# A layer's gradient passes through W2, W1 and Wo: products of rows already transposed first, row dots as soon as they can, the gelu slope made ahead, and the copies of these chains on ScalarE

## The chip, the cores and the metric

The kernel runs on one core of a Trainium2 chip. The metric is the time of one execution on the device, in microseconds (us). Lower is better. Each profile is of one run (for the kernel before, of one that is not in its median), so a trace's span and the median of the runs need not agree to the last microsecond.

The profile names the engines PE (TensorE matmuls), PEld (TensorE weight loads), DVE (VectorE), ACT (ScalarE), POOL (GpSimd) and SP (which issues loads).

## The reference

A decoder of four residual steps, attention, MLP, attention, MLP, with the same weights in both layers; then the gradient of everything by `grad_out`. There is one new token for each of two batch entries, so every matrix product has 2 columns, while the cache has 16384 positions. Cut to what matters:

```python
B, Sq, D = 2, 1, 1024;  Hq, Hkv, Sk, Dh = 32, 4, 16384, 128;  F = 3584

def attn(x, k_cache, v_cache, wq, wo):        # wq: D x 4096, wo: 4096 x D
    q = (x @ wq) ...                          # 32 heads, 8 to each cached head
    p = softmax(q k^T * Dh**-0.5)
    return (p v) ... @ wo
def mlp(x, w1, b1, w2, b2):
    y = layernorm(x)
    return gelu(y @ w1 + b1) @ w2 + b2

x = x + attn(layernorm(x), ...);  x = x + mlp(layernorm(x), ...)   # layer 0
x = x + attn(layernorm(x), ...);  x = x + mlp(layernorm(x), ...)   # layer 1
# outputs: x and, by jax.vjp, the gradients of x, k_cache, v_cache, wq, wo, w1, b1, w2, b2
```

## The kernel before

The kernel streams the caches through the core several times. Between the backward pass of layer 1's attention and the last stage (cache and weight gradients) lies a stretch in which one small vector, layer 0's gradient, must pass through everything in order:

- `dn` (the gradient that comes out of layer 1's attention), one layernorm backward, `gM_all`;
- W2 transposed (28 rows of 128), `dh_all`;
- W1 transposed, `dm_sb`;
- two layernorms backward, `gA_all`;
- Wo transposed (32 rows), `dof`, from which the last stage starts.

The weights lie in memory the wrong way round for this. A row of W2 or Wo is therefore "turned" first: eight 128x128 transposes on PE into an accumulator bank, one copy back by ScalarE or VectorE. Turning doesn't need the gradient, only the products of the row do. Every fifth row is not turned but "dotted": VectorE multiplies the row as it lies with the gradient spread over all partitions and sums, once for each batch entry. The spread itself is eight transposes and one copy for each batch entry. Rows of W2 have a second job, the forward product of layer 1 (into `fps`).

`pick` decides at build time which engine makes a copy: the one that has been charged less. The `hook` of `ln_bwd` puts PE work (rows to turn) into the wait for the cross-partition sum `part_sum`, which is itself a PE matmul.

```python
    load = {"A": 0.0, "D": 0.0}

    def charge(eng, us):
        load[eng] += us

    def pick():
        m = min(load.values())
        for k in load:
            load[k] -= m
        return "A" if load["A"] <= load["D"] else "D"

    def evac_bf16(dst, src, n):
        if pick() == "A":
            S.copy(out=dst.bitcast(I32), in_=src.bitcast(I32))
            charge("A", 0.17 + n / 2 / 1200.0)
        else:
            V.tensor_copy(out=dst, in_=src)
            charge("D", 0.16 + n / 1920.0)
    # ... cut ...
    def ln_bwd(dy, y, rstd, name, hook=lambda: None):
        t1 = wrk.tile([128, DJ, 2], F32, name="lb_t1")
        V.tensor_tensor(out=t1[:], in0=dy, in1=y, op=ALU.mult)
        s = small.tile([128, 2, 2], F32, name="lb_s")
        V.tensor_reduce(out=s[:, 0, :], in_=dy.rearrange("p j b -> p b j"), axis=AX.X, op=ALU.add)
        V.tensor_reduce(out=s[:, 1, :], in_=t1[:].rearrange("p j b -> p b j"), axis=AX.X, op=ALU.add)
        hook()
        ps = part_sum(s[:].rearrange("p a b -> p (a b)"), 4, "lb_ps")
        nm = small.tile([128, 2, 2], F32, name="lb_nm")
        V.tensor_scalar(out=nm[:].rearrange("p a b -> p (a b)"), in0=ps[:], scalar1=-1.0 / D, scalar2=None,
                        op0=ALU.mult)
        u = wrk.tile([128, DJ, 2], F32, name="lb_u")
        V.tensor_tensor(out=u[:], in0=y, in1=bcast_j(nm[:, 1, :], DJ), op=ALU.mult)
        V.tensor_tensor(out=u[:], in0=u[:], in1=dy, op=ALU.add)
        V.tensor_tensor(out=u[:], in0=u[:], in1=bcast_j(nm[:, 0, :], DJ), op=ALU.add)
        dx = wrk2.tile([128, DJ, 2], F32, name=name, tag="lb_dx")
        V.tensor_tensor(out=dx[:], in0=u[:], in1=bcast_j(rstd, DJ), op=ALU.mult)
        return dx
    # ... cut ...
    def turn(view, new_tp):

        tp = new_tp()
        for o in range(8):
            PE.transpose(tp[:, o, :], view[:, o * 128:(o + 1) * 128], ident[:])
        evac_bf16(view, tp[:].rearrange("p a b -> p (a b)"), 1024)

    class Dots:

        def __init__(self, name):
            self.rows = [ktp.tile([128, 2 * NB, 128], BF16, name=name, tag="blk", bufs=2) for _ in range(2)]
            self.junk = wrk.tile([128, D], BF16, name="junk", tag="rowout")

        def spread(self, b, col):
            tp = pt([128, 8, 128], BF16, "dotr")
            for o in range(8):
                PE.transpose(tp[:, o, :], col(o).to_broadcast([128, 128]), ident[:])
            evac_bf16(self.rows[b][:].rearrange("p a b -> p (a b)"), tp[:].rearrange("p a b -> p (a b)"), 1024)

        def dot(self, w, b, out):
            V.scalar_tensor_tensor(out=self.junk[:], in0=w, scalar=1.0, in1=self.rows[b][:].rearrange("p o d -> p (o d)"),
                                   op0=ALU.mult, op1=ALU.mult, accum_out=out)
            charge("D", 1.15)

    class Ahead:

        def __init__(self, W, n_in, name, xT_bf=None, fps=None):
            self.W, self.J, self.x, self.fps, self.name = W, n_in // 128, xT_bf, fps, name
            self.dotted = range(3, self.J, 5)
            self.dp = vec.tile([128, len(self.dotted), 2], F32, name=name + "_dp")
            self.chunks = list(w_chunks(n_in, D))
            self.rows = {}

        def load(self, k):
            j0, rb = self.chunks[k]
            wv = w_load(self.W, j0, rb, D)
            for j in range(rb):
                self.rows[j0 + j] = wv[:, j, :]

        def row(self, j):
            w = self.rows[j]
            if self.fps is not None:
                for jo in range(DJ):
                    PE.matmul(wide_out(self.fps, jo * WIDE), lhsT=w[:, jo * 128:(jo + 1) * 128],
                              rhs=wide_in(self.x[:, j, :]), start=False, stop=True, skip_group_check=True)
            if j not in self.dotted:
                turn(w, lambda: pt([128, 8, 128], BF16, "turn"))

        def spread(self, gT_bf):
            self.dd = Dots(self.name + "_g")
            for b in range(2):
                self.dd.spread(b, lambda o: gT_bf[:, o, b:b + 1])

        def products(self, j, out_ps, gT_bf):
            if j in self.dotted:
                for b in range(2):
                    self.dd.dot(self.rows[j], b, self.dp[:, self.dotted.index(j), b:b + 1])
                return
            for o in range(8):
                PE.matmul(wide_out(out_ps, 2 * j), lhsT=self.rows[j][:, o * 128:(o + 1) * 128],
                          rhs=wide_in(gT_bf[:, o, :]), start=(o == 0), stop=(o == 7))
    # ... cut ...
    def mlp_hidden_bwd(l, dhps, ahead=None):
        # ... cut: eight VectorE operations make the slope d1 of gelu from hpre and th ...
        V.tensor_tensor(out=dh_all[:, :, lsl(l)], in0=d1[:], in1=dhps[:], op=ALU.mult)
        if ahead is not None:
            V.tensor_tensor(out=dh_all[:, 3:FJ:5, lsl(l)], in0=d1[:, 3:FJ:5], in1=ahead.dp[:], op=ALU.mult)
    # ... cut ...
    charge("D", 2.0)
    g2 = attn_in_bwd(1, g3, dn1, lambda: some(rest, 2))
    V.tensor_copy(out=gM_all[:, :, lsl(0)], in_=g2[:])
    w2b.spread(gM_all[:, :, lsl(0)])
    some(rest, 6)
    dhps = px([128, 512], F32, "w2b_b")
    for j in range(FJ):
        some(rest, 1)
        w2b.products(j, dhps, gM_all[:, :, lsl(0)])
    mlp_hidden_bwd(0, pairs(dhps, FJ), w2b)
    x4 = mlp_out(1, fps[:, 0:DJ * WIDE].rearrange("p (j b) -> p j b", b=WIDE)[:, :, 0:2])
    sv = saved["m0"]
    _, dmps = w_pass(B_w1, D, F, "dm_ps", gT_bf=dh_all[:, :, lsl(0)],
                     mid=lambda: col_to_row_f32(x4, DJ, out_0.rearrange("b s d -> (b s) d"), "o0"))
    wob = Ahead(A_wo, HD, "wob")
    for k in range(len(wob.chunks)):
        wob.load(k)
    rest = deque(lambda j=j: wob.row(j) for j in range(wob.J - 4))
    dm = wrk.tile([128, DJ, 2], F32, name="dm_sb")
    V.tensor_copy(out=dm[:], in_=dmps[:])
    dn = ln_bwd(dm[:], sv["y2"][:], sv["rstd2"][:], "dn", lambda: some(rest, 4))
    dx = ln_bwd(dn[:], sv["y1"][:], sv["rstd1"][:], "dx", lambda: some(rest, 4))
    g1 = vec.tile([128, DJ, 2], F32, name="gM0")
    V.tensor_tensor(out=g1[:], in0=dx[:], in1=g2[:], op=ALU.add)
    V.tensor_copy(out=gA_all[:, :, lsl(0)], in_=g1[:])
    wob.spread(gA_all[:, :, lsl(0)])
    dops = px([128, 512], F32, "wob_b")
    for j in range(wob.J + 4):
        some(rest, 1)
        if j >= wob.J - 4 and j < wob.J:
            wob.row(j)
        if j >= 4:
            wob.products(j - 4, dops, gA_all[:, :, lsl(0)])
    TP = [pt([128, 8, 128], BF16, "tpm%d" % i) for i in range(2)]
    for t in TP:
        V.memset(t[:].bitcast(F32), 0.0)
    do_delta(0, pairs(dops, HQ), wob)
```

The copy of a turned row, when `pick` gives it to VectorE, lands in VectorE's order at the place where the row is turned, that is inside `ln_bwd` or ahead of the dots. In the timelines below VectorE works in the order of emission, so what stands behind such a copy waits with it. And a dot is emitted where the products of its row are, one row at a time.

Of the kernel before, what the change touches and what calls it, by code (L numbers as in the profile page):

```python
# [23 lines left out]
def kernel(  # L24
# [114 lines left out]

    def pick():  # L140
        m = min(load.values())
        for k in load:
            load[k] -= m
        return "A" if load["A"] <= load["D"] else "D"
# [73 lines left out]
    def ln_bwd(dy, y, rstd, name, hook=lambda: None):  # L218
# [6 lines left out]
        ps = part_sum(s[:].rearrange("p a b -> p (a b)"), 4, "lb_ps")  # L225
        nm = small.tile([128, 2, 2], F32, name="lb_nm")
# [109 lines left out]
    class Ahead:  # L336


        def __init__(self, W, n_in, name, xT_bf=None, fps=None):
            self.W, self.J, self.x, self.fps, self.name = W, n_in // 128, xT_bf, fps, name  # L340
            self.dotted = range(3, self.J, 5)
            self.dp = vec.tile([128, len(self.dotted), 2], F32, name=name + "_dp")
            self.chunks = list(w_chunks(n_in, D))
            self.rows = {}
# [20 lines left out]

        def products(self, j, out_ps, gT_bf):
            if j in self.dotted:
                for b in range(2):
                    self.dd.dot(self.rows[j], b, self.dp[:, self.dotted.index(j), b:b + 1])
                return  # L370
            for o in range(8):
                PE.matmul(wide_out(out_ps, 2 * j), lhsT=self.rows[j][:, o * 128:(o + 1) * 128],
                          rhs=wide_in(gT_bf[:, o, :]), start=(o == 0), stop=(o == 7))
# [210 lines left out]
    def attn_bwd(l, do_bf, dqT, dn, groups, ahead):  # L584
# [88 lines left out]
        while s < len(slots) + 2 or sch.busy():  # L673
            sch.s = s
            if s < len(slots):
# [3 lines left out]
                else:  # L679
# [3 lines left out]
                    if s % 3 == 2 and v_turns:  # L683
                        v_turns.popleft()()
# [103 lines left out]
    def mlp_hidden_bwd(l, dhps, ahead=None):  # L788
# [11 lines left out]
        d1 = wrk.tile([128, FJ, 2], F32, name="gb_d1")  # L800
        V.tensor_scalar(out=d1[:], in0=th[:], scalar1=1.0, scalar2=0.5, op0=ALU.add, op1=ALU.mult)
        V.tensor_tensor(out=d1[:], in0=d1[:], in1=x2[:], op=ALU.add)
        V.tensor_tensor(out=dh_all[:, :, lsl(l)], in0=d1[:], in1=dhps[:], op=ALU.mult)
        if ahead is not None:
            V.tensor_tensor(out=dh_all[:, 3:FJ:5, lsl(l)], in0=d1[:, 3:FJ:5], in1=ahead.dp[:], op=ALU.mult)
# [17 lines left out]
    def do_delta(l, dops, ahead=None):  # L823
        sv = saved[f"a{l}"]
        dof = wrk.tile([128, G, 8], F32, name="dof")
        for b in range(2):
            V.tensor_tensor(out=dof[:, b * HKV:(b + 1) * HKV, :].rearrange("p k r -> p (k r)"), in0=dops[:, :, b],
                            in1=sv["rbc"][:, b * HKV:(b + 1) * HKV, :].rearrange("p k r -> p (k r)"), op=ALU.mult)
            if ahead is not None:
                r_ = sv["rbc"][:, b * HKV:(b + 1) * HKV, :].rearrange("p k r -> p (k r)")  # L830
                V.tensor_tensor(out=dof[:, b * HKV:(b + 1) * HKV, :].rearrange("p k r -> p (k r)")[:, 3:HQ:5],
                                in0=ahead.dp[:, :, b], in1=r_[:, 3:HQ:5], op=ALU.mult)
# [55 lines left out]
    def attn_in_bwd(l, gT, dn, hook=lambda: None):  # L888
        sv = saved[f"a{l}"]
        dx = ln_bwd(dn[:], sv["y"][:], sv["rstd"][:], "dxa", hook)  # L890
# [12 lines left out]
    mlp_hidden(1, x3)  # L903

# [21 lines left out]

    charge("D", 2.0)
    g2 = attn_in_bwd(1, g3, dn1, lambda: some(rest, 2))
    V.tensor_copy(out=gM_all[:, :, lsl(0)], in_=g2[:])
    w2b.spread(gM_all[:, :, lsl(0)])  # L930
    some(rest, 6)
    dhps = px([128, 512], F32, "w2b_b")
    for j in range(FJ):
        some(rest, 1)
        w2b.products(j, dhps, gM_all[:, :, lsl(0)])
    mlp_hidden_bwd(0, pairs(dhps, FJ), w2b)
# [10 lines left out]
    dn = ln_bwd(dm[:], sv["y2"][:], sv["rstd2"][:], "dn", lambda: some(rest, 4))  # L947
    dx = ln_bwd(dn[:], sv["y1"][:], sv["rstd1"][:], "dx", lambda: some(rest, 4))
    g1 = vec.tile([128, DJ, 2], F32, name="gM0")
    V.tensor_tensor(out=g1[:], in0=dx[:], in1=g2[:], op=ALU.add)  # L950
    V.tensor_copy(out=gA_all[:, :, lsl(0)], in_=g1[:])
    wob.spread(gA_all[:, :, lsl(0)])
    dops = px([128, 512], F32, "wob_b")
    for j in range(wob.J + 4):
        some(rest, 1)
        if j >= wob.J - 4 and j < wob.J:
            wob.row(j)
        if j >= 4:
            wob.products(j - 4, dops, gA_all[:, :, lsl(0)])
# [358 lines left out]
    m = 0  # L1318
# [68 lines left out]
```

## Time and profile before

| | before |
|---|---|
| time, median (3 runs) | 1174.13 us (1173.18 to 1174.6) |
| bytes moved by DMA | 449.30 MB, 384 GB/s over the span |
| `dn` to `dh_all` (norm and W2) | 27.49 us |
| `dh_all` to `dm_sb` (W1) | 23.06 us |
| `dm_sb` to `gA_all` (two norms) | 5.99 us |
| `gA_all` to `dof` (Wo) | 22.71 us |
| `dof` to the end (last stage) | 419.5 us |

The last five rows are differences of start times in the timeline of VectorE. From the page of the kernel before, the span and the busy times of the engines:

```profile
span 1171.5 us, 39963 instructions
PE 967.2 (83%) x17565; PEld 738.7 (63%) x17565; DVE 639.2 (55%) x1342; ACT 562.9 (48%) x1412; POOL 63.7 (5%) x113
```

No engine is full over the whole span. The DMA is, in most of it (a share of 0.99 up to 660 us and 0.98 from 850 us to the end), and nearly so beside W2 and W1 (a share of 0.84 at 676 to 700 us, 1.00 at 700 to 722), but not beside Wo. Windows of the kernel before (columns as its first line says; PEclk is the granted TensorE clock as a share of full speed):

```profile
core 0: us, PE busy (x) PEld busy (x) DVE busy (x) ACT busy (x) POOL busy (x), PEclk, DMA share, GB/s
730.00:740.00 10.00, 9.84 (x184) 9.33 (x182) 6.83 (x11) 5.37 (x10) 0.00 (x0) 0.84 0.06 10
740.00:750.00 10.00, 7.09 (x194) 6.66 (x190) 9.72 (x17) 4.57 (x8) 0.00 (x0) 1.00 1.03 391
```

At 730 to 740 us almost nothing is loaded (a share of 0.06), since no buffer comes free before rows of Wo are done with: in the waits of SP the last load of Wo waits 16.5 us, for a dot. Time in this stretch is a chain of waits, not bandwidth. VectorE's timeline of the kernel before, from `dm_sb` on (start, duration, engine, line, operation, output and inputs; in brackets the idle time before it and what ended that):

```profile
723.27 0.17 DVE L946 COPY dm_sb<-dm_ps_b 128x16 f32<-128x16 f32 x1 [1.44 <-PE dm_ps_b L274]
...
723.79 0.69 DVE L151 COPY wt<-turn 128x1024 bf16<-128x1024 bf16 x1
725.18 0.69 DVE L151 COPY wt<-turn 128x1024 bf16<-128x1024 bf16 x1 [0.70 <-PE turn L315]
725.79 0.15 DVE L227 TENSOR_SCALAR lb_nm<-lb_ps 128x4 f32<-128x4 f32 x1
...
727.13 0.69 DVE L151 COPY wt<-turn 128x1024 bf16<-128x1024 bf16 x1
728.02 0.16 DVE L227 TENSOR_SCALAR lb_nm<-lb_ps 128x4 f32<-128x4 f32 x1 [0.20 <-PE lb_ps L178]
...
729.26 0.17 DVE L951 CAST gA_all<-gM 128x16 bf16<-128x16 f32 x1
730.30 0.69 DVE L151 COPY wob_g<-dotr 128x1024 bf16<-128x1024 bf16 x1 [0.87 <-PE dotr L328]
732.09 0.69 DVE L151 COPY wt<-turn 128x1024 bf16<-128x1024 bf16 x1 [1.10 <-PE turn L315]
733.65 0.69 DVE L151 COPY wt<-turn 128x1024 bf16<-128x1024 bf16 x1 [0.87 <-PE turn L315]
735.08 0.69 DVE L151 COPY wt<-turn 128x1024 bf16<-128x1024 bf16 x1 [0.73 <-PE turn L315]
735.68 1.22 DVE L332 SCALAR_TENSOR_TENSOR junk<-wt,wob_g 128x1024 bf16<-128x1024 bf16 x1
...
749.69 1.22 DVE L332 SCALAR_TENSOR_TENSOR junk<-wt,wob_g 128x1024 bf16<-128x1024 bf16 x1
751.03 1.03 DVE L962 MEMSET tpm<- 128x512 f32 x2
751.97 0.17 DVE L827 TENSOR_TENSOR dof<-wob_b,rbc 128x32 f32<-128x32 f32 x1
```

The twelve dots follow each other without a gap from 735.68 us to the memsets and `dof`, so VectorE is what ends last in Wo. What can be won is the start of the first dot, 6.42 us after `gA_all`. In those 6.42 us VectorE makes four copies and waits before each of them for PE to transpose (0.87, 1.10, 0.87 and 0.73 us). Only the first of them, of the spread, is one that the dots need from VectorE. In the norms the copy at 725.18 us stands ahead of `lb_nm` in the same way: it waits 0.70 us for a turn that has nothing to do with the norm.

In W2 it is PE that ends last. VectorE's timeline of the kernel before around W2:

```profile
672.72 0.17 DVE L877 TENSOR_TENSOR dn<-dn,dn_ps 128x16 f32<-128x16 f32 x1 [1.91 <-PE dn_ps L875]
...
676.42 0.17 DVE L929 CAST gM_all<-gA 128x16 bf16<-128x16 f32 x1
...
697.41 0.21 DVE L792 TENSOR_TENSOR gb_t<-th 128x56 f32<-128x56 f32 x1
...
700.21 0.21 DVE L803 TENSOR_TENSOR dh_all<-gb_d,w2b_b 128x56 bf16<-128x56 f32 x1 [1.17 <-PE w2b_b L372]
```

The gelu slope (first operation at 697.41 us, line L792) is done 1.17 us before PE's last product, for which `dh_all` waits. So the slope at this place costs nothing. PE in turn waits once for the gradient, in the waits of PE between 672 and 702 us (us in total, times, longest):

```profile
PE dotr L328 <- DVE gM_all L929: 1.5, 1, 1.5
```

### The profile page before, as it was taken

The numbers are of one execution on the slowest core, as the hardware profiler recorded it, in microseconds if no ns is written. First come the engines' busy times: TensorE is split into PE (matmuls) and PEld (weight loads), VectorE is DVE, ScalarE is ACT, GpSimd is POOL, SyncE is SP. The second block draws the span as 40 slices with busy tenths as digits, with TensorE's granted clock in tenths as the row PEclk, the third lists the DMA queues.
The fourth block names the chain that finished last, engine by engine and source line by source line (L and its number), as shares of the span: only waits on it lengthen the run. The fifth ranks groups of instructions, "written<-read, shape, count | busy, mean of one in ns | idle before, by whom it ended". The sixth has DMA issues, their size and how long they took to land. (4 is left out here: it accounts for less than half of the span.)

```text
span 1171.5 us, 39963 instructions
## 1 busy us (share of the span) xinstructions
PE 967.2 (83%) x17565; PEld 738.7 (63%) x17565; DVE 639.2 (55%) x1342; ACT 562.9 (48%) x1412; POOL 63.7 (5%) x113
## 2 busy tenths in 40 slices
PE   4989796487879976899987788688898989999885
PEld 3867674487767755887775688555555554555552
DVE  1544341133545423454844454757877768796784
ACT  0544351022535420344454454367767757686673
POOL 0000000000000000000000000001111111111111
PEclk9988885597989875899997999888878767796885
DMA  9999999998999989999999989667999999999996
GB/s 370 418 419 418 419 419 397 395 352 367 419 419 418 417 306 418 375 351 403 364 412 412 341 319 344 253 263 297 375 418 420 418 413 421 420 420 418 423 424 265
DMA packets 89130, 449.30 MB, mean 384 GB/s; under 512 B 7026, under 2 KB 7026, under 8 KB 49788
## 3 DMA queue, kind: packets, MB, share of 16 engines
q1 hardware_dynamic: 72204, 348.17, 74.4%
q0 software_dynamic: 16752, 98.59, 20.5%
q8 instruction: 137, 2.24, 0.8%
q14 instruction: 37, 0.30, 0.1%
HBM read 348.14 MB, written 98.58 MB: 381 GB/s over the span
## 5 line engine op out<-in xcount | busy, mean ns | idle before, releaser
L148 ACT COPY kT<-tp 128x512 int32<-128x512 int32 x206 | 120.8, 586 | 256.7 <-PE tp L411 248.9
L151 DVE COPY kT<-tp 128x1024 bf16<-128x1024 bf16 x162 | 110.9, 691 | 117.6 <-PE tp L411 110.5
L411 PE MATMUL tp<-ident,kv_K 128*128 128x128 bf16 x1728 | 144.8, 233 | 5.0 <-DMA kv_K<-in_A_k_cache_dram 3.9
L411 PEld LDWEIGHTS <-kv_K 128*128 128x128 bf16 x1728 | 109.9, 104 | 5.8 <-DMA kv_K<-in_A_k_cache_dram 5.0
L159 DVE CAST big<-xm 128x512 bf16<-128x512 f32 (+1 forms) x137 | 89.4, 686 | 27.2 <-PE xm L1189 12.4
L156 ACT CAST big<-xm 128x512 bf16<-128x512 f32 (+1 forms) x160 | 87.1, 593 | 25.1 <-PE xm L1048 13.3
L564 PEld LDWEIGHTS <-kT 128*128 128x128 bf16 x2048 | 76.6, 98 | 28.5 <-issue 22.9
L564 PE MATMUL sc<-qT_bf,kT 128*128 128x8 bf16 x2048 | 92.0, 171 | 0.1
L263 PE MATMUL wtp<-ident,wt 128*128 128x128 bf16 x928 | 78.4, 234 | 4.5 <-issue 3.3
L411 PE MATMUL tp<-ident,kv_V 128*128 128x128 bf16 x864 | 69.8, 227 | 9.7 <-DMA kv_V<-in_A_v_cache_dram 8.4
L528 ACT ACTIVATE e_all<-sc,negm 128x64 bf16<-128x64 f32 x256 | 76.9, 343 | 1.2 <-DVE negm L523 1.0
L299 PEld LDWEIGHTS <-wt 128*128 128x128 bf16 x1696 | 49.1, 104 | 44.6 <-issue 14.9
L443 PE MATMUL acc_all<-kv_V,e_all 128*16 128x256 bf16 x864 | 47.4, 300 | 27.8 <-DMA kv_V<-in_A_v_cache_dram 14.0
L159 DVE CAST keepK<-xm 128x512 bf16<-128x512 f32 x94 | 61.0, 685 | 16.7 <-PE xm L1189 12.7
L148 ACT COPY wT<-wtp 128x512 int32<-128x512 int32 (+1 forms) x63 | 36.1, 575 | 70.4 <-PE wtp L263 60.3
L151 DVE COPY wT<-wtp 128x1024 bf16<-128x1024 bf16 (+1 forms) x61 | 38.4, 634 | 52.5 <-PE wtp L263 48.3
L156 ACT CAST keepK<-xm 128x512 bf16<-128x512 f32 x103 | 55.6, 592 | 22.1 <-PE xm L1189 20.5
L263 PEld LDWEIGHTS <-wt 128*128 128x128 bf16 x928 | 60.3, 105 | 5.1 <-issue 3.8
L411 PEld LDWEIGHTS <-kv_V 128*128 128x128 bf16 x864 | 55.3, 102 | 11.3 <-DMA kv_V<-in_A_v_cache_dram 9.1
L156 ACT CAST keepV<-xm 128x512 bf16<-128x512 f32 (+1 forms) x98 | 52.8, 595 | 19.0 <-PE xm L1189 17.7
L528 ACT ACTIVATION_READ_ACCUMULATOR e_all<-sc,negm 128x1 f32 x256 | 59.9, 234 | 0.0
L159 DVE CAST keepV<-xm 128x512 bf16<-128x512 f32 (+1 forms) x74 | 48.3, 686 | 18.0 <-PE xm L1189 13.4
(345 smaller groups left out, 1793.2 us busy)
## 6 DMA issues: line engine op xcount, KB each, us to landing
kv_K<-in_A_k_cache_dram SPq DMA_DIRECT2D x81, 1024.0 KB, 12.6
kv_V<-in_A_v_cache_dram SPq DMA_DIRECT2D x81, 1024.0 KB, 12.3
out_dram<-big POOLq DMA_DIRECT2D x36, 1024.0 KB, 18.5
wt<-in_A_wo_dram SPq DMA_DIRECT2D x32, 1024.0 KB, 10.1
wt<-in_B_w_dram SPq DMA_DIRECT2D x32, 896.0 KB, 14.4
out_dram<-keepK POOLq DMA_DIRECT2D x22, 1024.0 KB, 17.5
out_dram<-keepV POOLq DMA_DIRECT2D x18, 1024.0 KB, 16.4
wt<-in_A_wq_dram SPq DMA_DIRECT2D x16, 1024.0 KB, 9.0
```

The source lines that it names most:

```text
L148: S.copy(out=dst.bitcast(I32), in_=src.bitcast(I32))
L151: V.tensor_copy(out=dst, in_=src)
L156: S.copy(out=dst, in_=src)
L159: V.tensor_copy(out=dst, in_=src)
L263: PE.transpose(tp[:, o, :], wv[:, j, (o0 + o) * 128:(o0 + o + 1) * 128], ident[:])
L299: PE.matmul(fps[:, jo, :].rearrange("p (a b) -> p a b", b=2), lhsT=wv[:, j, jo * 128:(jo + 1) * 128], rhs=xT_bf[:, j0 + j, :].unsqueeze(1) ...
L411: PE.transpose(tp[:, j, :], cv[:, b * 8 + j, :], ident[:])
L443: PE.matmul(self.acc[cg:cg + 16, :], lhsT=coef(u), rhs=self.cv[:, t:t + 2, :].rearrange("p t d -> p (t d)"), start=False, stop=True, tile_ ...
L528: S.activation(out=e_all[:, g, f * half:(f + 1) * half, l, h, :], in_=sc[g][f][:, h, :].rearrange("p (a b) -> p a b", b=2), func=ACT.Exp, ...
L564: PE.matmul(sc[g][f][:, :, t % TH], lhsT=kT[:, j, :], rhs=q_bf[:, g, :], start=True, stop=True)
```

## The change

Its intent: give each gradient something to do at once. Rows that are already turned get their products as soon as the gradient is there, ahead of the spread. Dots are emitted apart from products, so that those of loaded rows come in one go. Rows are moved behind `part_sum` (the new `after`), so that the sum starts earlier. The slope is made ahead of the norm. While all this runs, every copy is ScalarE's (`only`), so that VectorE's order holds only the chain and the dots. Some turns of V move away from the first steps of a loop. The diff, cut to its core:

```diff
+    only = {"e": None}
+
     def pick():
+        if only["e"]:
+            return only["e"]
         m = min(load.values())
 # ... ln_bwd:
         hook()
         ps = part_sum(s[:].rearrange("p a b -> p (a b)"), 4, "lb_ps")
+        after()
 # ... Ahead:
-            self.dotted = range(3, self.J, 5)
+            self.dotted = range(4, self.J, 5)
+        def dots(self, j):
+            for b in range(2):
+                self.dd.dot(self.rows[j], b, self.dp[:, self.dotted.index(j), b:b + 1])
+
         def products(self, j, out_ps, gT_bf):
             if j in self.dotted:
-                for b in range(2):
-                    self.dd.dot(self.rows[j], b, self.dp[:, self.dotted.index(j), b:b + 1])
                 return
 # ... the backward pass of attention:
-                    if s % 3 == 2 and v_turns:
+                    if s % 3 == 2 and s >= 8 and v_turns:
                         v_turns.popleft()()
 # ... mlp_hidden_bwd is split: mlp_slope(l) makes d1, the rest uses it
 # ... W2:
-    charge("D", 2.0)
-    g2 = attn_in_bwd(1, g3, dn1, lambda: some(rest, 2))
+    mlp_slope(0)
+    only["e"] = "A"
+    g2 = attn_in_bwd(1, g3, dn1, lambda: some(rest, 2), lambda: some(rest, 3))
     V.tensor_copy(out=gM_all[:, :, lsl(0)], in_=g2[:])
+    dhps = px([128, 512], F32, "w2b_b")
+    turned = 5
+    for j in range(4):
+        w2b.products(j, dhps, gM_all[:, :, lsl(0)])
     w2b.spread(gM_all[:, :, lsl(0)])
-    some(rest, 6)
-    dhps = px([128, 512], F32, "w2b_b")
-    for j in range(FJ):
-        some(rest, 1)
+    w2b.dots(4)
+    for j in range(4, FJ):
+        for _ in range(2 if turned < j + 5 else 1):
+            if turned < FJ:
+                some(rest, 1)
+                if turned in w2b.dotted:
+                    w2b.dots(turned)
+                turned += 1
         w2b.products(j, dhps, gM_all[:, :, lsl(0)])
+    only["e"] = None
     mlp_hidden_bwd(0, pairs(dhps, FJ), w2b)
 # ... norms and Wo:
-    dn = ln_bwd(dm[:], sv["y2"][:], sv["rstd2"][:], "dn", lambda: some(rest, 4))
-    dx = ln_bwd(dn[:], sv["y1"][:], sv["rstd1"][:], "dx", lambda: some(rest, 4))
+    only["e"] = "A"
+    dn = ln_bwd(dm[:], sv["y2"][:], sv["rstd2"][:], "dn", lambda: some(rest, 2), lambda: some(rest, 3))
+    dx = ln_bwd(dn[:], sv["y1"][:], sv["rstd1"][:], "dx", lambda: some(rest, 1), lambda: some(rest, 4))
     V.tensor_copy(out=gA_all[:, :, lsl(0)], in_=g1[:])
+    dops = px([128, 512], F32, "wob_b")
+    for j in range(4):
+        wob.products(j, dops, gA_all[:, :, lsl(0)])
     wob.spread(gA_all[:, :, lsl(0)])
-    dops = px([128, 512], F32, "wob_b")
-    for j in range(wob.J + 4):
-        some(rest, 1)
-        if j >= wob.J - 4 and j < wob.J:
-            wob.row(j)
-        if j >= 4:
-            wob.products(j - 4, dops, gA_all[:, :, lsl(0)])
+    for j in wob.dotted:
+        if j < wob.J - 4:
+            wob.dots(j)
+    turned = 10
+    for j in range(4, wob.J):
+        # ... cut: turn one more row (with its dots, if it is a late dotted one), then
+        wob.products(j, dops, gA_all[:, :, lsl(0)])
+    only["e"] = None
```

More of the change, by code (lines that the diff above doesn't have):

```diff
@@ L216, in ln_fwd, with ln_bwd @@
         return y, rstd
-    def ln_bwd(dy, y, rstd, name, hook=lambda: None):
+    def ln_bwd(dy, y, rstd, name, hook=lambda: None, after=lambda: None):
         t1 = wrk.tile([128, DJ, 2], F32, name="lb_t1")
@@ L786, in mlp_out, with mlp_slope @@
         return xn
-    def mlp_hidden_bwd(l, dhps, ahead=None):
+    def mlp_slope(l):
         sv = saved[f"m{l}"]
@@ L799, in mlp_hidden_bwd @@
         V.tensor_tensor(out=x2[:], in0=x2[:], in1=t2[:], op=ALU.mult)
-        d1 = wrk.tile([128, FJ, 2], F32, name="gb_d1")
+        d1 = sv["d1"] = vec.tile([128, FJ, 2], F32, name=f"gb_d1{l}")
         V.tensor_scalar(out=d1[:], in0=th[:], scalar1=1.0, scalar2=0.5, op0=ALU.add, op1=ALU.mult)
         V.tensor_tensor(out=d1[:], in0=d1[:], in1=x2[:], op=ALU.add)
+    def mlp_hidden_bwd(l, dhps, ahead=None):
+        d1 = saved[f"m{l}"]["d1"]
         V.tensor_tensor(out=dh_all[:, :, lsl(l)], in0=d1[:], in1=dhps[:], op=ALU.mult)
         if ahead is not None:
-            V.tensor_tensor(out=dh_all[:, 3:FJ:5, lsl(l)], in0=d1[:, 3:FJ:5], in1=ahead.dp[:], op=ALU.mult)
+            V.tensor_tensor(out=dh_all[:, 4:FJ:5, lsl(l)], in0=d1[:, 4:FJ:5], in1=ahead.dp[:], op=ALU.mult)
     def mlp_in_bwd(l, gT):
@@ L830, in do_delta @@
                 r_ = sv["rbc"][:, b * HKV:(b + 1) * HKV, :].rearrange("p k r -> p (k r)")
-                V.tensor_tensor(out=dof[:, b * HKV:(b + 1) * HKV, :].rearrange("p k r -> p (k r)")[:, 3:HQ:5],
-                                in0=ahead.dp[:, :, b], in1=r_[:, 3:HQ:5], op=ALU.mult)
+                V.tensor_tensor(out=dof[:, b * HKV:(b + 1) * HKV, :].rearrange("p k r -> p (k r)")[:, 4:HQ:5],
+                                in0=ahead.dp[:, :, b], in1=r_[:, 4:HQ:5], op=ALU.mult)
         doT_bf = vec.tile([128, G, 8], BF16, name=f"doT_bf{l}")
@@ L886, in wq_steps, with attn_in_bwd @@
         return [lambda j=j: load(j) for j in (0, 4)], dq_in, [lambda j=j: turn_row(j) for j in range(DJ)], products, box
-    def attn_in_bwd(l, gT, dn, hook=lambda: None):
+    def attn_in_bwd(l, gT, dn, hook=lambda: None, after=lambda: None):
         sv = saved[f"a{l}"]
-        dx = ln_bwd(dn[:], sv["y"][:], sv["rstd"][:], "dxa", hook)
+        dx = ln_bwd(dn[:], sv["y"][:], sv["rstd"][:], "dxa", hook, after)
         gn = vec.tile([128, DJ, 2], F32, name=f"gA{l}")
@@ L903 @@
     mlp_hidden(1, x3)
+    mlp_slope(1)
     mlp_hidden_bwd(1, dh_up1)
@@ L951 @@
     V.tensor_copy(out=gA_all[:, :, lsl(0)], in_=g1[:])
+    dops = px([128, 512], F32, "wob_b")
+    for j in range(4):
+        wob.products(j, dops, gA_all[:, :, lsl(0)])
     wob.spread(gA_all[:, :, lsl(0)])
-    dops = px([128, 512], F32, "wob_b")
-    for j in range(wob.J + 4):
-        some(rest, 1)
-        if j >= wob.J - 4 and j < wob.J:
-            wob.row(j)
-        if j >= 4:
-            wob.products(j - 4, dops, gA_all[:, :, lsl(0)])
+    for j in wob.dotted:
[3 more added lines that the diff above has]
+    for j in range(4, wob.J):
+        if j >= 10 or j % 2 == 0:
+            if turned < wob.J - 4:
+                some(rest, 1)
+            elif turned < wob.J:
+                wob.row(turned)
+                if turned in wob.dotted:
+                    wob.dots(turned)
+            turned += 1
+        wob.products(j, dops, gA_all[:, :, lsl(0)])
+    only["e"] = None
     TP = [pt([128, 8, 128], BF16, "tpm%d" % i) for i in range(2)]
```

## The prediction

> **What bounds the kernel now.** The span is 1171.5 us. The slices view shows the DMA at 418-423 GB/s over most of it; by stretches, it is 1.00 busy from about 820 us on and again before 660 us. Between lies a serial stretch, about 672 to 757 us, where layer 0's gradient passes through W2, W1 and Wo. There transfers only follow freed buffers (DMA share 0.06 at 730-740 us). The change works there. What it shortens, I expect to move the DMA-bound remainder earlier by as much; it saves no bytes.
>
> By the timeline this stretch has three parts:
> - W2 (672.5-700.2): PE is last. It idles 1.5 us for gM_all; part_sum comes about 1.1 us after lb_s, behind the two rows of the hook. Dots end at 697.5 and the gelu slope (8 VectorE operations, 1.65 us) at 699.05, before PE: neither is critical.
> - W1 (700-722.9): PE-bound, unchanged.
> - two layer norms and Wo (722.9-756): PE ends at 748.2, the 12 row dots (1.22 us each, every 1.27 us) at 750.9, then two memsets, then the delta chain at 751.97. VectorE is last: its first dot starts only at 735.7, 6.3 us after gA_all (729.4), behind copies and rows.
>
> **What the change does.**
> 1. W2. Rows 2-4 fill PE's idle time after part_sum: up to -1.5 us. But the order of instructions puts the 8 slope operations between dn and lb_t, in the gradient's chain. [...] they delay it by 1.65 us; the two hook rows on PE hide about 1.1 us. Net about -1.0 us. Taking the slope off the end gains nothing while PE is last.
> 2. W1. ScalarE was charged for all forced copies, so VectorE gets the first six copies (0.69 us each, against about 0.63 us of PE work a unit): +0.6 us.
> 3. Layer norms. Fewer rows before each part_sum (2 and 1, not 4 and 4) and no VectorE copies inside: lb_nm about 1.4 us earlier in the first; gA_all about 1.5 us earlier after both.
> 4. Wo. Products of rows 0-3, then the spread; dots start about 2.1 us after gA_all instead of 6.3 and run without gaps: 12 x 1.27 = 15.2 us. Dots end about 5.75 us earlier relative to the start of the norms (items 3 and 4 together). ScalarE's 18 remaining copies (about 0.6 us each) and PE (transposes 0.41 us, products 0.2 us a row[...]) should end 1-3 us before the dots.
> 5. Moving the early turns of V: about -0.3 us. The final stage's start gets more VectorE copies: about neutral.
>
> Sum: -1.0 + 0.6 - 5.75 - 0.3 = about -6.4 us; I take 6.
>
> **Predicted: 1168 us, 1164.5 to 1171.5 (8 in 10).** Faster by over 2%: 0.02; within 2%: 0.97; slower: 0.01.
>
> **What would show it.** gM_all no earlier than before (about 0.6 us later after dn); slope operations between dn and lb_t; first Wo dot about 2.1 us after gA_all; dots without gaps and still last; the final stage (first keepV product after colsV) about 6 us earlier; DMA share over 0.5 at 730-740 us, as Wo rows are freed earlier; shares after 850 us unchanged.
>
> **What would make it wrong.** PE's mid-row stalls without a releaser (1.0-1.8 us, one per 256 weight loads) growing when DMA is busier; ScalarE becoming last in Wo; the final stage absorbing the gain because its transfers do not move with it; a different granted clock.

The sum stands at -1.0 + 0.6 - 5.75 - 0.3 = -6.45, written as about -6.4 us, of which 6 was taken. That the slope delays the chain by its whole 1.65 us (697.41 to 699.05 us in the kernel before) is the author's estimate. In the same trace, where the clock is 1.00, eight transposes of a row take 0.44 us (736.47 to 736.91) and eight products 0.20 us (736.26 to 736.47); the stalls of PE without a releaser took 0.80, 1.73, 0.34, 0.92 and 1.00 us between 684 and 748 us (the weight loads between them are counted in the last section).

## The result, and the profile after

| | before | after |
|---|---|---|
| median of the runs made together (4 each) | 1174.37 us (1173.18 to 1175.61) | 1164.26 us (1162.77 to 1167.13) |
| ratio, 95% interval | | 0.9917 (0.9894 to 0.994) |

A ratio compares the mean times of the two kernels' fast runs of the same rounds, so it is not quite the ratio of the medians quoted. The result is within 2%, as predicted. The median lies 0.24 us below the low end of the predicted range, 1164.5; two later measurements of the same kernel gave 1165.42 and 1164.21 us. The profiled run of the kernel after was the slowest of its four. Its span and busy times:

```profile
span 1165.4 us, 39945 instructions
PE 955.5 (82%) x17565; PEld 733.2 (63%) x17565; DVE 639.5 (55%) x1344; ACT 562.3 (48%) x1410; POOL 63.9 (5%) x113
```

The work is the same within a few microseconds of any engine, and the bytes are the same 449.30 MB. Windows of the kernel after:

```profile
core 0: us, PE busy (x) PEld busy (x) DVE busy (x) ACT busy (x) POOL busy (x), PEclk, DMA share, GB/s
730.00:740.00 10.00, 9.92 (x241) 9.51 (x237) 9.72 (x17) 8.38 (x15) 0.00 (x0) 1.00 1.03 378
740.00:750.00 10.00, 3.62 (x55) 2.45 (x53) 7.47 (x31) 0.28 (x1) 0.00 (x0) 0.61 0.69 287
```

At 730 to 740 us VectorE now has 9.72 us of work where it had 6.83, and the DMA is full where it had been idle: rows of Wo are freed earlier. The stage as a whole also moved, so count from `gA_all` instead: in the first and second 5 us behind it the DMA share was 0.05 and 0.01 before, and is 0.61 and 1.02 after. The last load of Wo now waits 6.6 us, for products, where it waited 16.5 us for a dot. VectorE's timeline of the kernel after, from `dm_sb` on:

```profile
720.24 0.17 DVE L967 COPY dm_sb<-dm_ps_b 128x16 f32<-128x16 f32 x1 [0.83 <-PE dm_ps_b L279]
...
721.32 0.16 DVE L232 TENSOR_SCALAR lb_nm<-lb_ps 128x4 f32<-128x4 f32 x1 [0.49 <-PE lb_ps L182]
...
723.43 0.16 DVE L232 TENSOR_SCALAR lb_nm<-lb_ps 128x4 f32<-128x4 f32 x1 [0.70 <-PE lb_ps L182]
...
724.68 0.17 DVE L973 CAST gA_all<-gM 128x16 bf16<-128x16 f32 x1
727.05 1.23 DVE L337 SCALAR_TENSOR_TENSOR junk<-wt,wob_g 128x1024 bf16<-128x1024 bf16 x1 [2.20 <-ACT wob_g L152]
...
741.06 1.23 DVE L337 SCALAR_TENSOR_TENSOR junk<-wt,wob_g 128x1024 bf16<-128x1024 bf16 x1
742.40 1.03 DVE L995 MEMSET tpm<- 128x512 f32 x2
743.34 0.17 DVE L837 TENSOR_TENSOR dof<-wob_b,rbc 128x32 f32<-128x32 f32 x1
```

No copy is left in VectorE's order. `lb_nm` waits only for its own sum, the first dot only for the spread (2.20 us), 2.37 us after `gA_all`. From the first dot to `dof` it takes 16.29 us, before as after (751.97 - 735.68 and 743.34 - 727.05). The whole gain of this part, 28.70 - 23.10 = 5.60 us from `dm_sb` to `dof`, is made before the first dot. Around W2, in the kernel after:

```profile
671.53 0.17 DVE L887 TENSOR_TENSOR dn<-dn,dn_ps 128x16 f32<-128x16 f32 x1 [1.91 <-PE dn_ps L885]
671.62 0.21 DVE L799 TENSOR_TENSOR gb_t<-th 128x56 f32<-128x56 f32 x1
...
673.05 0.22 DVE L809 TENSOR_TENSOR gb_d<-gb_d,gb_x 128x56 f32<-128x56 f32 x1
673.18 0.17 DVE L224 TENSOR_TENSOR lb_t<-dn,a_y 128x16 f32<-128x16 f32 x1
...
675.38 0.17 DVE L941 CAST gM_all<-gA 128x16 bf16<-128x16 f32 x1
...
698.44 0.21 DVE L813 TENSOR_TENSOR dh_all<-gb_d,w2b_b 128x56 bf16<-128x56 f32 x1 [8.06 <-PE w2b_b L379]
```

The slope now stands between `dn` and `lb_t`, in the chain; and `dh_all` waits 8.06 us for PE's last product where it waited 1.17. Nothing was gained at that end.

### The profile page after: what moved, and what is told of

Same layout as the page of the kernel before. It is cut to its first block, busy times and chain, and to the rows that moved or that the text cites. A ratio compares the mean times of both kernels' runs of the same rounds, so it can differ in the third digit from the quotient of the medians.

```text
span 1165.4 us, 39945 instructions
## 1 busy us (share of the span) xinstructions
PE 955.5 (82%) x17565; PEld 733.2 (63%) x17565; DVE 639.5 (55%) x1344; ACT 562.3 (48%) x1410; POOL 63.9 (5%) x113
## 2 busy tenths in 40 slices
DMA packets 89130, 449.30 MB, mean 386 GB/s; under 512 B 7026, under 2 KB 7026, under 8 KB 49788
## 5 line engine op out<-in xcount | busy, mean ns | idle before, releaser
L155 DVE COPY wT<-wtp 128x1024 bf16<-128x1024 bf16 (+1 forms) x65 | 41.5, 645 | 48.7 <-PE wtp L268 45.2
L152 ACT COPY wT<-wtp 128x512 int32<-128x512 int32 (+1 forms) x59 | 33.5, 568 | 69.2 <-PE wtp L268 60.5
L160 ACT CAST keepV<-xm 128x512 bf16<-128x512 f32 (+1 forms) x91 | 49.4, 594 | 34.9 <-PE xm L1222 28.8
L163 DVE CAST keepV<-xm 128x512 bf16<-128x512 f32 (+1 forms) x81 | 52.8, 685 | 18.1 <-PE xm L1222 14.1
```

The source lines that it names most:

```text
L160: S.copy(out=dst, in_=src)
```

## The experiments

The theory (A): the gain is made where VectorE's order is freed of copies, in the norms and Wo; W2, W1, the slope and the turns of V are worth about nothing. Rivals: the W2 part gives a good share of it (B); or the earlier turns of V or the last stage does, since a single trace of each kernel can't tell a gain from the scatter between traces.

Twelve runs were made, in three calls, each call on one chip with its own runs of the kernel before. All were correct.

| kernel | median us | before in its call | ratio | 95% interval |
|---|---|---|---|---|
| x1: turns of V as before | 1166.74 | 1171.75 | 0.9955 | 0.9931 to 0.998 |
| x2: norms and Wo changed, W2 as before | 1166.45 | 1171.75 | 0.9951 | 0.9932 to 0.9971 |
| x3: W2 changed, norms and Wo as before | 1172.07 | 1171.75 | 0.9996 | 0.9972 to 1.002 |
| x4: change, copies shared as before | 1172.88 | 1171.75 | 1.0013 | 0.9987 to 1.0039 |
| c0: the change again | 1165.42 | 1171.65 | 0.9956 | 0.9936 to 0.9975 |
| w1: before, ScalarE copies in norms and Wo | 1167.39 | 1171.65 | 0.9958 | 0.9942 to 0.9975 |
| y1: change, slope late | 1165.73 | 1171.65 | 0.995 | 0.9937 to 0.9963 |
| z3: combined version | 1164.41 | 1171.65 | 0.9944 | 0.9927 to 0.9962 |
| c1: the kernel before again | 1173.64 | 1175.84 | 0.9977 | 0.9954 to 1.0001 |
| c2: the change, third time | 1164.21 | 1175.84 | 0.991 | 0.9893 to 0.9927 |
| d1: the change, chain made longer | 1179.2 | 1175.84 | 1.0034 | 1.0015 to 1.0054 |
| z3 again | 1164.86 | 1175.84 | 0.9902 | 0.9883 to 0.9922 |

Before any of it is read, look at c1: the kernel before, unaltered, against itself came out at 0.9977. So a ratio of one call is uncertain by about a quarter of a per cent, some 3 us, and the change itself measured 0.9917, 0.9956 and 0.991. The durations between points of the traces are much finer in the stretch from `dm_sb` to `dof`. In us:

| kernel | `dn` to `gM_all` | `dn` to `dm_sb` | of it W1 | `dm_sb` to `gA_all` | `gA_all` to first dot | `gA_all` to `dof` | `dm_sb` to `dof` | `dof` to end |
|---|---|---|---|---|---|---|---|---|
| before | 3.70 | 50.55 | 23.06 | 5.99 | 6.42 | 22.71 | 28.70 | 419.5 |
| c1 (before) | 3.70 | 50.14 | 22.48 | 6.00 | 6.46 | 22.73 | 28.73 | 419.6 |
| after | 3.85 | 48.71 | 21.80 | 4.44 | 2.37 | 18.66 | 23.10 | 422.1 |
| c0 (after) | 3.93 | 46.60 | 21.64 | 4.43 | 2.38 | 18.66 | 23.09 | 423.8 |
| c2 (after) | 3.94 | 47.88 | 21.90 | 4.44 | 2.37 | 18.65 | 23.09 | 417.7 |
| x1 | 3.74 | 47.55 | 21.44 | 4.44 | 2.37 | 18.65 | 23.09 | 419.5 |
| x2 | 2.73 | 47.23 | 20.70 | 4.43 | 2.37 | 18.66 | 23.09 | 421.6 |
| x3 | 3.75 | 47.13 | 21.91 | 6.16 | 6.22 | 22.49 | 28.65 | 419.8 |
| x4 | 5.90 | 49.14 | 21.63 | 9.04 | 3.59 | 19.80 | 28.84 | 421.0 |
| w1 | 3.71 | 48.72 | 20.11 | 5.71 | 1.50 | 17.79 | 23.50 | 423.1 |
| y1 | 3.71 | 47.26 | 21.71 | 4.44 | 2.36 | 18.65 | 23.09 | 420.7 |
| z3 | 2.72 | 46.83 | 21.63 | 4.44 | 1.76 | 16.92 | 21.36 | 424.5 |
| z3 again | 3.70 | 48.69 | 21.77 | 4.43 | 1.77 | 16.93 | 21.36 | 424.1 |
| d1 | 3.73 | 47.80 | 21.64 | 4.43 | 2.38 | 31.63 | 36.06 | 422.4 |

From `dm_sb` to `dof`, traces of one arrangement agree to 0.05 us. From `dn` to `dm_sb`, and from `dof` to the end, they scatter by microseconds. That decides what can be settled from one trace and what can't.

### The turns of V (x1)

```diff
-                    if s % 3 == 2 and s >= 8 and v_turns:
+                    if s % 3 == 2 and v_turns:
```

Expected:

> The changed kernel with one part undone: the turns of the kept V tiles start at slot 2 again. The traces show dn (the last add before the W2 stretch) 1.2 us earlier in the changed kernel than in the kernel before. Theory A: moving the turns made that 1.2 us; then dn comes at about 672.7 us here, the stretch after it keeps the changed kernel's length (dn to the first dof 71.8 us), and the time is about 1 us above the changed kernel's (ratio to before about 0.9925 against 0.9917). Rival: the 1.2 us are run-to-run variation of the DMA-bound part; then dn is anywhere between 671 and 673 and the time equals the changed kernel's within 0.15%.

Measured: 0.9955, against 0.9956 of the whole change in the second call. `dn` begins at 673.10 us, inside the scatter of the three traces of the change (670.44 to 673.18). The turns of V do nothing that these runs can see.

### One half of the change each (x2, x3)

x2 has W2 of before (dotted rows from 3, its hook of two rows, spread first, one row and its products at a time, slope at the end) and the new norms and Wo; x3 the reverse. The core of x2:

```diff
-    mlp_slope(0)
-    only["e"] = "A"
-    g2 = attn_in_bwd(1, g3, dn1, lambda: some(rest, 2), lambda: some(rest, 3))
+    charge("D", 2.0)
+    g2 = attn_in_bwd(1, g3, dn1, lambda: some(rest, 2))
 # ... W2's loop of before, then
+    mlp_slope(0)
```

and of x3:

```diff
-    only["e"] = "A"
-    dn = ln_bwd(..., "dn", lambda: some(rest, 2), lambda: some(rest, 3))
-    dx = ln_bwd(..., "dx", lambda: some(rest, 1), lambda: some(rest, 4))
+    dn = ln_bwd(..., "dn", lambda: some(rest, 4))
+    dx = ln_bwd(..., "dx", lambda: some(rest, 4))
 # ... and Wo's loop of before
```

> The changed kernel with the W2 part undone (order of rows, dots, slope and shared copies as before in W2; row 3 dotted there), the norms and Wo as changed. Theory A (the gain is the shorter serial chain, mostly from the norms and the dots on VectorE): dn to dm_sb about 50.5 us as before, dm_sb to the first dof 23.1 us as in the changed kernel (28.7 before), time about 1174.1 - 5.6 - 1.2 = 1167.3 us, ratio 0.994. Rival B (the gain comes from W2's rows being freed earlier, so that W1 and Wo land earlier): most of the gain is lost, ratio above 0.997.

> The changed kernel with the norms and the Wo part undone, the W2 part as changed. Theory A: dn to dm_sb about 48.7 us as in the changed kernel (50.5 before), dm_sb to the first dof 28.7 us as before, time about 1174.1 - 1.8 - 1.2 = 1171.1 us, ratio 0.9974. Rival B: it keeps most of the gain, ratio below 0.994.

Measured: x2 0.9951 and x3 0.9996, with x1, that has both parts, at 0.9955. From `dm_sb` to `dof`, x2 has all of the gain (23.09 us) and x3 none (28.65). This decides for A and against B as far as the intervals reach: the norms and Wo carry the time, and W2's part alone is not seen in it. But W2's part may still be worth one or two microseconds, which these intervals can't show (below). One number of x2's expectation missed: with the old W2, `dn` to `dm_sb` took 47.23 us and not 50.5, so the length of that stretch in the first trace of the kernel before was not the old order's doing alone.

### The change without copies kept to ScalarE (x4)

```diff
-    only["e"] = "A"      # at both places
+    only["e"] = None
```

> The changed kernel with one part undone: the copies in both chains are shared between ScalarE and VectorE again; order of rows, products and dots as changed. Theory A (VectorE's dots end last in Wo, so each copy of 0.69 us that VectorE takes before or among them delays the delta chain): dm_sb to the first dof grows from 23.1 us by 0.7 us per VectorE copy, about 3 to 5 copies, so to 25 to 26.5 us, and the time is 2 to 3.5 us above the changed kernel's (ratio 0.994 to 0.995). Rival C (the order of products and dots made the gain, and it does not matter who copies): dm_sb to the first dof stays within 0.7 us of 23.1 us and the ratio at 0.992.

Measured: 1.0013, and 28.84 us from `dm_sb` to `dof`. The expectation for this stretch, 25 to 26.5 us, missed: not a part of the gain is lost but all of it. VectorE's timeline of x4, second norm:

```profile
724.70 0.69 DVE L155 COPY wt<-turn 128x1024 bf16<-128x1024 bf16 x1 [1.11 <-PE turn L320]
726.50 0.69 DVE L155 COPY wt<-turn 128x1024 bf16<-128x1024 bf16 x1 [1.10 <-PE turn L320]
727.11 0.15 DVE L232 TENSOR_SCALAR lb_nm<-lb_ps 128x4 f32<-128x4 f32 x1
```

What I had not seen is that `after` makes it worse. The rows behind `part_sum` are emitted ahead of `lb_nm`; any of their copies that falls to VectorE stands ahead of it too and waits for those rows to be turned (four of them in the second norm). `dm_sb` to `gA_all` takes 9.04 us, against 5.99 in the kernel before and 4.44 in the change. So `after` is only good together with ScalarE's copies. In Wo, x4 keeps a part of the gain (19.80 us against 22.71).

### Only ScalarE's copies (w1)

The reverse: the kernel before, in its old order, with `only` set around the norms and Wo and nothing else.

```diff
+    only["e"] = "A"
     dn = ln_bwd(dm[:], sv["y2"][:], sv["rstd2"][:], "dn", lambda: some(rest, 4))
 # ... Wo as before
+    only["e"] = None
```

> The kernel before with one part of the change alone: in the norms and in Wo all copies on ScalarE; hooks of 4 and 4 rows, spread, rows, products and dots in the old order. Theory A (the copies made most of the gain in Wo; the order of rows made that in the norms): dm_sb to gA_all stays near 6.0 us (4.4 in the changed kernel), the first dot comes about 2.2 us after gA_all instead of 6.4 and the dots run without gaps, so gA_all to the first dof is about 18.5 us (18.66 changed, 22.7 before); dm_sb to the first dof about 24.5 us, time about 4 us below before (ratio 0.9965). Rival C (moving dots ahead of products made the gain): the first dot still waits for its place in the row loop, gA_all to the first dof stays above 21 us.

Measured: 0.9958, as the whole change in the same call (0.9956), and 23.50 us from `dm_sb` to `dof`: 5.20 us of the 5.60 are had by this edit alone, more than expected (24.5 us), and rival C, by which the first dot would still wait for its place in the row loop, falls. VectorE's timeline of w1:

```profile
727.51 0.17 DVE L956 CAST gA_all<-gM 128x16 bf16<-128x16 f32 x1
729.01 1.23 DVE L336 SCALAR_TENSOR_TENSOR junk<-wt,wob_g 128x1024 bf16<-128x1024 bf16 x1 [1.33 <-ACT wob_g L152]
```

The first dot starts 1.50 us after `gA_all`, earlier than in the change (2.37). That splits the rest. In the norms the new order of rows is worth 5.71 - 4.44 = 1.27 us. In Wo the new order costs 18.66 - 17.79 = 0.87 us: the products of rows 0 to 3, which the change puts ahead of the spread, hold up the transposes that the first dot waits for, and the dots are what ends last. z3 (below) takes that away and wins back 0.60 us of the 0.87 (first dot 1.77 us after `gA_all`); in its trace the transposes then start 0.50 us after `gA_all`, behind rows emitted behind `part_sum`, against 0.23 us in w1, which is the other 0.27. "Products at once" delays VectorE, which had no time to spare. It does free rows earlier: the last load of Wo waits 6.6 us in the change and 10.8 us in w1. That the dots are now emitted in one go changes nothing that I can see: with no copies on VectorE, its order is dot after dot in either case (argued from the order of instructions; no run has it alone).

### The slope (y1)

```diff
-    mlp_slope(0)                      # ahead of the norm
     ...
     only["e"] = None
+    mlp_slope(0)                      # ahead of mlp_hidden_bwd, as before
     mlp_hidden_bwd(0, pairs(dhps, FJ), w2b)
```

> The changed kernel with the gelu slope back behind the dots. Theory A (made ahead it sits in the gradient's chain, dn to lb_t, and gains nothing behind the dots, where VectorE waited 8 us for PE): dn to gM_all shorter by 0.8 to 1.2 us (3.75 to about 2.8), dn to dh_all shorter by 0.3 to 0.8 us, no later dh_all; time within 0.1% of the changed kernel's. Rival (the slope made ahead is worth its 1.65 us): dn to dh_all longer by about 1.6 us.

Measured: 0.995 against 0.9956, which is the same. `dn` to `gM_all` took 3.71 us, hardly less than in the change (3.85 to 3.94); what I expected of taking eight operations out of it missed, and `dn` to `dh_all` was no shorter either (25.55 us, c0 24.96). The traces of all kernels with this step, sorted by the mean granted clock between `dn` and `gM_all`, show why:

| `dn` to `gM_all`, us | full clock (1.00) | lower clock |
|---|---|---|
| slope late | 2.72 (z3), 2.73 (x2) | 3.70 (before, at 0.66), 3.70 (c1, 0.68), 3.71 (w1, 0.50), 3.71 (y1, 0.66), 3.70 (z3 again, 0.68) |
| slope ahead | 3.74 (x1), 3.75 (x3), 3.73 (d1) | 3.85 (after, 0.69), 3.93 (c0, 0.57), 3.94 (c2, 0.68) |

So the slope in the chain costs 1.0 us of this step at full clock, and 0.15 to 0.24 us at a lower one, where the two rows of the hook on PE take nearly as long as the slope does and hide it: with the slope late, `lb_nm` waits 0.89 us for its sum in z3 (clock 1.00) and 1.88 us in y1 (mean clock 0.66) and in the kernel before, where the clock is 0.50 in the first 2 us. (x4 is left out: its VectorE makes copies here.) At full clock the microsecond seems to reach `dh_all`; see W2 below.

### A version combined from this (z3, twice)

The slope late; the spread ahead of the products in Wo; the two banks that the last stage needs cleared by ScalarE, which has little to do there (0.28 us of work from 740 to 750 us in the kernel after), in place of VectorE's memsets ahead of `dof`; and the charges of `pick` set to zero behind both forced stretches.

```diff
+    load["A"] = load["D"] = 0.0      # behind both only["e"] = None
+    mlp_slope(0)                     # behind W2, as in y1
+    wob.spread(gA_all[:, :, lsl(0)])
     for j in range(4):
         wob.products(j, dops, gA_all[:, :, lsl(0)])
-    wob.spread(gA_all[:, :, lsl(0)])
     for t in TP:
-        V.memset(t[:].bitcast(F32), 0.0)
+        S.activation(out=..., in_=onesf[:]..., func=ACT.Copy, scale=0.0)
```

> A proposed better version: the changed kernel with the slope behind the dots; in Wo the spread ahead of the products of rows 0 to 3; the two clears of the transposition banks on ScalarE instead of VectorE; and the balance of copies reset to zero after each of the two chains. Theory A: gA_all to the first dof shorter by 0.85 us (spread) and 1.0 us (clears), 18.66 to about 16.8 us; the W1 pass (dh_all to dm_sb) about 0.5 us shorter than the changed kernel's 21.4 to 21.9; in sum 2.5 to 3 us below the changed kernel of this call, ratio lower by about 0.0023. If ScalarE and PE, which ended 1.6 us ahead of the dots, become last instead, gA_all to dof stays above 17.3 us.

> The proposed better version a second time beside the changed kernel. Expected: gA_all to the first dof 16.9 us again; time 1.7 us below the changed kernel of this call if the span follows the stretch, ratio lower by 0.0015, hardly clear of noise in one call.

Measured: VectorE's timeline of z3, in its first run:

```profile
726.58 0.17 DVE L974 CAST gA_all<-gM 128x16 bf16<-128x16 f32 x1
...
742.35 1.22 DVE L337 SCALAR_TENSOR_TENSOR junk<-wt,wob_g 128x1024 bf16<-128x1024 bf16 x1
743.50 0.18 DVE L837 TENSOR_TENSOR dof<-wob_b,rbc 128x32 f32<-128x32 f32 x1
```

`dof` now follows the last dot directly. The stretch from `dm_sb` to `dof` is 21.36 us in both traces, 1.73 us less than in the change. The ratios are 0.9944 and 0.9902, lower than those of the change in the same calls by 0.0012 and 0.0008, about 1 us each. That fits, and it is the lowest ratio in both calls, but it isn't clear of the noise, and of the 0.0023 expected in the first call about half came. Nothing shows it to be slower.

z3 also tested the W1 step of the prediction, that ScalarE's charges from the forced stretch push W1's first copies onto VectorE and cost 0.6 us. With the charges set to zero W1 as a whole did not move: 21.63 and 21.77 us, with them 21.44 to 21.91. But the reason does not fall with that. In the timelines ScalarE makes the first seven copies of W1 in the kernel before, VectorE the first three in the change (not six), and in z3 they take turns from the first. And PE's waits that nothing released ("issue" in the profile) differ between these traces. Without them W1 took 20.70 and 20.65 us in z3, 20.93 in y1, which has z3's late slope with the charges, and 21.07 to 21.16 in the three traces of the change and in d1. So about 0.25 us seems to hang on the charges; in z3 it was covered by longer stalls (0.93 and 1.12 us, against 0.52 to 0.78).

### The chain made longer on purpose (d1), and controls (c0, c1, c2)

Does a microsecond of the chain reach the end of the kernel, or does the last stage, whose DMA share is 0.98 from 850 us to the end before and after, take it back? d1 clears the two banks 13 times over, ahead of `dof`, which leaves the results right.

```diff
-    for t in TP:
+    for t in TP * 13:
         V.memset(t[:].bitcast(F32), 0.0)
```

> A dose: the changed kernel with 24 more clears of the transposition banks on VectorE ahead of the delta chain, at about 0.5 us each by the trace, 12.4 us in all; results stay correct. Theory P (the span follows the length of the serial stretch one to one, whatever the last stage's own variation): time 12.4 us above the changed kernel of this call, ratio higher by 0.0106. Rival Q (the last stage, bound by transfers, absorbs a part because its loads run ahead in the meantime): less than 8 us, ratio higher by less than 0.007.

> The changed kernel itself, unaltered, as a control on the same chip as the other runs of this call. Expected: dm_sb to the first dof 23.1 us as in its first trace; dn to dm_sb 47.1 to 48.7 us depending on the granted clock and PE's mid-row stalls; ratio to before 0.992 if the first measurement was typical, about 0.995 if the earlier runs with V's turns or W2 undone (0.9955 and 0.9951) show what this chip state gives for nearly the same kernel.

> The kernel before, unaltered, as a control with its own trace. Expected: dm_sb to the first dof 28.7 us again (it has been the same within 0.02 us in every trace of one program order). For dn to dm_sb, two theories: if the 50.55 us of the first trace came from the granted clock (0.80 at 672-680 us and 0.87 at 700-710 us, 1.00 in most later traces), it is 47.5 to 49 us in a trace with full clock; if the W2 part of the change shortens it, it stays above 50 us. Ratio 1.000.

> The changed kernel a third time, to settle its size: the first measurement gave a ratio of 0.9917 (4 runs of each), the control 0.9956 (6 runs). Theory: the true gain is the 5.6 us of the norms and Wo, ratio 0.995 to 0.9955, and the first pair was a favourable draw of the last stage; rival: W2's part is worth another 3 to 4 us on the right chip, ratio 0.992.

Measured: VectorE's timeline of d1:

```profile
742.21 14.00 DVE L995 MEMSET tpm<- 128x512 f32 x26
756.11 0.18 DVE L837 TENSOR_TENSOR dof<-wob_b,rbc 128x32 f32<-128x32 f32 x1
```

The memsets grew from 1.03 to 14.00 us, the chain by 36.06 - 23.09 = 12.97 us. The ratio rose from 0.991 (c2) to 1.0034, which is 0.0124 x 1175.84 = 14.6 us; the medians differ by 15.0. So a lengthening of the chain reaches the end in full, within the noise, and the rival by which the last stage absorbs it falls. For the direction of the change the first call is the test: the two kernels with the short chain (x1, x2) have a mean median 5.9 us below the two with the long one (x3, x4), for 5.6 us of chain, and the last stage took as long behind the one (419.5, 421.6 us) as behind the other (419.8, 421.0). (A memset of 128x512 took 14.00 / 26 = 0.54 us.)

The controls give the size of the noise used above: the change is 0.9917, 0.9956 and 0.991, the kernel before against itself 0.9977. Two expectations missed here. c2 was to give 0.995 to 0.9955; 0.991 is nearer to its rival's 0.992. The traces of c1 and c2, 11.3 us apart, differ by 1.5 us before `dn`, 2.3 from `dn` to `dm_sb`, 5.6 from there to `dof` and 1.9 in the last stage, and only the third of these comes out alike in every pair of traces of the two kernels. And c1 could not decide what made `dn` to `dm_sb` long in the first trace, since its clock was below full there again (0.95 in W1).

## Why the prediction was right or wrong

**The sum was right, and the term that carries it was right to 0.15 us.** Predicted for the norms and Wo together: 5.75 us. Measured: 5.60, with a range of 0.05 in the traces. Its parts hold too: `gA_all` about 1.5 us earlier after the start of the norms (measured 5.99 - 4.44 = 1.55); first dot about 2.1 us after `gA_all` (measured 2.37); dots without gaps and still last; a DMA share over 0.5 at 730 to 740 us (measured 1.03); the last stage about 6 us earlier (`dof` moved from 751.97 to 743.34, 8.6 us, of which 1.2 came before `dn` and 1.8 in W2 and W1). The mechanism, as these traces show it: work emitted ahead of an operation of the chain on VectorE held it up. A copy that waited 0.70 us for PE stood ahead of `lb_nm` at 725.18 us in the kernel before, and x4 shows two more with 1.1 us each. The slope, emitted ahead of `lb_t`, did so in the same way: `lb_t` started 1.65 us after `dn` in the kernel after (673.18 - 671.53), and 0.20 us after it in the kernel before (672.92 - 672.72). x2, x3, w1 and x4 show that this is where the time is.

**What does the winning is narrower than the change.** The prediction gave the gain to items 3 and 4 as wholes. By w1 the choice of the engine for the copies gives 5.20 of 5.60 us; the new order of rows adds 1.27 us in the norms and takes 0.87 back in Wo.

**W2 and W1, predicted -1.0 + 0.6: W2 was mis-sized.** From `dn` to `dm_sb` six traces with W2's new arrangement (after, c0, c2, x1, x3, d1) took 46.6 to 48.7 us, mean 47.6; four with the old one (before, c1, w1, x2) 47.2 to 50.6, mean 49.2. That is about -1.5 us in place of -0.4, but the two ranges overlap, and the clock is mixed into it: at 676 to 700 us three of the four with the old order had a granted clock of 0.98, 0.96 and 0.86, x2 1.00; the six with the new one 0.93 to 1.00. Where the clock was 1.00 from 672 to 722 us, the old order took 47.23 us (x2) and the new one 47.55 and 47.13 (x1, x3): no gain.

The same traces, with z3's first, also split the sum, if PE's waits that nothing released (1.74 to 2.70 us in W2) are taken off. `dn` to `dh_all` then took 24.02 us in x2, 23.59 and 23.48 in x1 and x3, and 22.50 in z3, which has the new order and the slope late. So filling the 1.5 us for which PE waited is worth about 1.5 us, as predicted, and the slope in the chain takes 1.0 back, where the prediction had 0.55: the step that was off is "the two hook rows on PE hide about 1.1 us", which at full clock hide about 0.6 of the slope's 1.65. W2 comes to -0.5 in place of -1.0. W1, taken in the same way, took 20.48 us in x2 and 20.93 and 21.09 in x1 and x3: +0.5 or +0.6, as predicted, with VectorE taking the first two or three copies, not six. How much of that is the copies' doing stays open (z3 above). These are one or two traces of each kind: seen, not shown.

**The slope.** That it would stand in the chain was right, and that taking it off the end gains nothing was right (y1). That `gM_all` would come about 0.6 us later after `dn` was too much for the first pair of traces (3.85 - 3.70 = 0.15) and too little at full clock (1.0); the prediction had one figure where the clock decides.

**The turns of V**, predicted -0.3 us, gave nothing measurable (x1).

**The median was lower than predicted**, by 3.7 us (1164.26 against 1168). The medians of the change lie 10.1, 6.2 and 11.6 us below those of the kernel before in the same call, so how near the predicted 6 us a call comes is in part luck. The three ratios of the change have a mean of (0.9917 + 0.9956 + 0.991) / 3 = 0.9928, which is 0.0072 x 1174 = 8.5 us. The traces account for 5.6 (shown) and at most about 1.5 more (the means above, which at equal clock show nothing); the 1.4 to 2.9 that are left are about the quarter of a per cent by which the kernel before differs from itself. The last stage is no explanation: it was 417.7 to 423.8 us in the three traces of the change and 419.5 and 419.6 in the two of the kernel before, so if anything longer.

## What to carry to other kernels

When an engine is the last one in a chain, look at its order of instructions for work that waits for someone else: here seven copies of 0.69 us brought 4.3 us of waiting with them beside 4.8 us of work, and giving them to the other engine was worth nearly all that a large rewrite brought. Put first what the last engine's first instruction needs (the spread), not what the engine with time to spare could do at once (the products). And before a gain of a per cent is split into parts, run the unaltered kernel against itself and read parts from durations between fixed points of the traces, not from times.

## What else the traces show, without a cause

- In the kernel after, the granted clock (third number from the end) stayed at 0.50 over the 15 us of these windows, while PE was busy for 78 to 90% of each and waited up to 0.52 us at a time. Why it did not rise is not shown:

```profile
747.40:752.40 5.00, 4.46 (x81) 2.86 (x82) 2.78 (x11) 0.00 (x0) 0.00 (x0) 0.50 0.04 13
752.40:757.40 5.00, 3.88 (x60) 2.01 (x56) 3.21 (x6) 2.39 (x5) 0.00 (x0) 0.50 0.00 0
757.40:762.40 5.00, 4.48 (x84) 2.14 (x84) 1.60 (x3) 1.81 (x4) 0.58 (x1) 0.50 0.52 213
```

- PE's timeline of the kernel after shows two stalls in the middle of a row, with no one waited for, 0.69 and 1.60 us long:

```profile
684.59 0.49 PE L361 MATMUL w2b_f<-h_all,wt 128*128 128x32 bf16 x13 [0.69 <-issue]
...
690.80 0.30 PE L379 MATMUL w2b_b<-gM_all,wt 128*128 128x32 bf16 x5 [1.60 <-issue]
```

  In this trace 128 weight loads and 128 matmuls lie between the two; in the kernel before, three stretches from one such stall to the next hold 256 weight loads each (12.00, 11.30 and 12.80 us), the next one 385 (22.9 us). The two of the kernel after lie in W2, where PE ends last (`dh_all` waits 8.06 us for it). Their cause is not shown; no run takes them away.
- One unaltered kernel measured against itself came out at 0.9977 with an interval of 0.9954 to 1.0001, and the last stage took 417.7 to 423.8 us in three traces of the same kernel.
